# A fused attention and silu feed-forward kernel: block sums and the splits of v in another order, two silus in one, fourth sums queued behind the next first

## The chip, the cores and the metric

The kernel runs on one core of a Trainium2 chip. The metric is device time in microseconds for one execution; a kernel's time is the median over its runs.

## The reference, cut to what matters

```python
def _attn_ref(q, k, v, tau):                    # q, k, v: (2, 6016, 256) f32
    qn = q / (norm(q, axis=1) + 1e-6); kn = k / (norm(k, axis=1) + 1e-6)
    a = softmax(kn.transpose(0, 2, 1) @ qn / tau)       # (2, 256, 256): over channels
    return v @ a
def _moe_ref(x, w_in, w_out):                   # (12032, 256) @ (256, 2048) @ (2048, 256)
    h = x @ w_in
    return (h * (1 / (1 + exp(-h)))) @ w_out
```

The output is `_moe_ref(attention(q, k, v), w_in, w_out)`, a 12032 x 256 array.

## The kernel before

The attention matrix is only 256 x 256 for each of the two batches, so the kernel folds it into `w_in` (`mix`, line 433) and never forms the attention's output: tokens of v go straight into the first matmul. What is left is two matrix products with a silu between them. Both are done in a Strassen-like scheme of seven products for a 2 x 2 block product, and every f32 factor is split into a high and a low f16 half, so that one product is three matmuls (high x low, low x high, high x high).

Tokens are worked on in twelve "pairs" of up to 1024 columns (`pairs`, line 477; six for a batch, the last of a batch 896). Pairs 0 and 5 go through `emit_pair_group` (line 648), the other ten through `emit_unit` (line 706). A pair has eight units (`u` 0 to 7; the first four make the output of one half of the columns, `t` = 0, the last four the other). A unit has four slots, each ended by a `yield`:

- slot 0: products into the PSUM banks y, x and z; copies of y (`c5`) and x (`c1`) by ScalarE; `tail(0)`; the first subtraction, `top[:, 0]` = c1 - z.
- slot 1: products added to y and x; the copy `c2` of x; silu of `top[:, 0]`; `tail(1)`; the second subtraction, `top[:, 1]` = c2 - y.
- slot 2: a product (S3, T3) added to x; the third subtraction, `low[:, 1]` = x - c5; silu of `top[:, 1]`; `tail(2)`.
- slot 3: a product (A22, T4) added to x; `tail(3)`; silu of `low[:, 1]`; the last silu, from x; `high` (line 735) makes the high f16 half of the two top blocks. Then `out_of_unit` (line 795) registers what remains for later slots.

Bank x is used by four products of a unit in turn, and each one but the first needs what the one before it left to have been read.

`later(slot, ...)` (line 786) puts closures into a table by tick, a tick being one slot, and `tail` (line 780) runs those of the present tick in the order in which they were registered. For unit u these are, in the slots of unit u + 1: slot 0 `rest_top` (the low half of the top blocks, line 739, the "upper rest"), `first_sum` and `high_low`; slot 1 `rest_low` and `third_sum` (t3 = b12 + b22); slot 2 `other_sums` (t2 = t3 + b11, t4 = t2 + b21). When a half of the columns ends (u = 3 or 7) four `take`s follow in ticks 4 to 7 (ScalarE reads a finished output bank), `join` in tick 7 and two `leave`s in ticks 10 and 11 (VectorE, then a DMA on SP).

The first sum t1 = b11 + b12 and the fourth sum t4 are made by DMA: a plain DMA of the first block and an accumulating DMA of the second one, both on the POOL queue, where the second waits for the first to land (lines 910 and 911; 922 and 923). At the end of a half t4 is made by VectorE instead, and at the very end t1 too.

The output matmuls of a unit stand in the list `ready`, in passes of four matmuls with cost 4: seven in `now`, then those in `then`, which need the sums t2, t3, t1, and the fourth sum t4 of the unit before (`behind_one`). After each slot's products the main loop (line 1266) takes passes for a cost of 8, 12, 16 and 8 in slots 0 to 3. TensorE works them off in that order.

In the ten pairs the order on TensorE, VectorE and ScalarE is that of the program (`tc.manual_schedule`, line 1217); pairs 0 and 5 are ordered by the scheduler. POOL and SP each have a queue of their own.

In the background `scale_v` (line 490) prepares the next pair's v: the maximum of its absolute values by four reductions (line 518, `amax_of`), a scale (`pow2_scale`, one small matmul), sums and differences of v's blocks in f32, and the splits (`put`, line 523, by lines 163 and 165: ScalarE makes the high half, VectorE in the same step the low one). Each `yield` is a step; lines 1275 to 1278 take one in slots 0, 2 and 3 of units 1 to 7. In pairs 1 to 3 `square_sums` (line 246) runs one square of k or q in slot 1 (line 1282). In pair 0 the weights are decoded (`decode`, line 188) with a scratch tile from the room of six g buffers that the unit's blocks use too.

## Time and profile before

| | us |
|---|---|
| median of 3 runs | 1072.84 |
| lowest and highest run | 1068.92, 1073.32 |
| the profiled execution, its own time | 1070.59 |
| its span, first to last instruction | 1068.8 |
| TensorE busy in the span | 1017.0 |
| VectorE busy in the span | 826.9 |
| ScalarE busy in the span | 811.4 |

All rows below are of the profiled execution. Times are microseconds from the start of the span. PE is TensorE, DVE VectorE, ACT ScalarE, POOL GpSimd, SP SyncE; L719 is line 719 of the kernel. Names like `x<-m,wall` are tiles: what is written, and what it is made of. "Idle before" is the time for which an engine stood still ahead of an instruction, and behind the arrow stands what ended it. Ends of matmuls are modelled.

### The profile page before, as it was taken

To read this page: it belongs to the slowest core of one execution; us is meant where nothing else is said; L and a number is where in the kernel's file an instruction comes from. 1 tells how busy PE (TensorE), PEld (TensorE's weight loads), DVE (VectorE), ACT (ScalarE), POOL (GpSimd) and SP (SyncE) were. 2 spreads that over 40 slices of the span, in tenths; PEclk is the share of its full clock that TensorE was granted. 3 is DMA by queue.
4 is the path that set the end of the run, shared out by engine and by line. 5 is a ranking of instruction groups with operands and counts; after the bars stand their busy time and mean duration, and the time that the engine had idled before them with its cause. 6 is when DMAs were issued, how large, how long until landed. Compare 5 with 4: busy or idle time off the path is not lost.

```text
span 1068.8 us, 20527 instructions
## 1 busy us (share of the span) xinstructions
PE 1017.0 (95%) x8222; PEld 839.8 (79%) x8222; DVE 826.9 (77%) x1358; ACT 811.4 (76%) x1241; POOL 210.5 (20%) x301
## 2 busy tenths in 40 slices
PE   9999999998999999999999999999999999999986
PEld 8876545887888888887655787888888888888985
DVE  6998486777878778878778878878878878877764
ACT  6688596887887788778778677777777777777763
POOL 1011000222222222222000122222222222222331
PEclk9999999999999999999999999999999999999998
DMA  9995010647647556435200346435435445445443
GB/s 369 396 399 174 1 40 4 189 117 230 157 121 234 141 130 177 119 80 159 50 1 5 120 95 163 101 99 158 119 88 151 119 99 142 116 96 125 110 110 82
DMA packets 62897, 143.81 MB, mean 135 GB/s; under 512 B 6930, under 2 KB 19314, under 8 KB 62802
## 3 DMA queue, kind: packets, MB, share of 16 engines
q0 software_dynamic: 32048, 73.02, 29.3%
q1 hardware_dynamic: 30466, 68.95, 18.1%
q8 instruction: 64, 1.05, 0.4%
q10 hardware_dynamic: 288, 0.52, 0.1%
q14 instruction: 31, 0.25, 0.1%
HBM read 57.67 MB, written 12.32 MB: 65 GB/s over the span
## 4 chain that ended last, share of the span: by engine, by line
PE 50%; DVE 16%; ACT 14%; issue 10%; DMA 7%; POOL 2%; POOLq 0%; DVEq 0%; ACTq 0%
PE o L830 18%; PE x L719 10%; PE o L627 5%; PE sc L300 5%; PE y L719 4%; DVE hl L739 4%; ACT hl L736 4%; DVE g L726 4%; DMA sums<-t 3%; DMA sums<-hl 3%; ACT g L729 3%; ACT m L163 2%; PE x L658 2%; PE z L719 2%; DVE t L904 2%
## 5 line engine op out<-in xcount | busy, mean ns | idle before, releaser
L719 PEld LDWEIGHTS <-wall 128*128 128x128 f16 x3360 | 327.5, 98 | 67.6 <-issue 32.4
L719 PE MATMUL x<-m,wall 128*128 128x256 f16 (+1 forms) x1920 | 259.1, 271 | 22.0 <-DVE g L726 13.9
L739 DVE SCALAR_TENSOR_TENSOR hl<-g,sg,hl 128x1024 f16<-128x1024 f32 (+1 forms) x160 | 202.7, 1267 | 67.1 <-ACT hl L736 66.2
L830 PE MATMUL o<-hl,wo 128*128 128x256 f16 (+1 forms) x1920 | 248.5, 273 | 0.8 <-DVE hl L739 0.8
L830 PEld LDWEIGHTS <-wo 128*128 128x128 f16 x2240 | 220.0, 98 | 25.9 <-issue 1.1
L729 ACT ACTIVATE g<-g,alpha 128x512 f32<-128x512 f32 (+1 forms) x240 | 170.1, 716 | 86.0 <-DVE g L726 85.7
L736 ACT ACTIVATE hl<-g,sg 128x1024 f16<-128x1024 f32 (+1 forms) x160 | 181.6, 1136 | 0.0
L719 PE MATMUL y<-m,wall 128*128 128x256 f16 (+1 forms) x960 | 129.6, 271 | 0.1
L911 POOL DMA_DIRECT2D sums<-hl x79 | 67.9, 859 | 248.8 <-DMA sums<-hl 191.9
L910 POOL DMA_DIRECT2D sums<-hl x79 | 55.0, 697 | 264.1 <-DVE hl L739 99.4
L923 POOL DMA_DIRECT2D sums<-hl x60 | 53.8, 896 | 198.2 <-ACT hl L736 30.2
L756 ACT COPY c<-x 128x512 f32<-128x512 f32 (+1 forms) x80 | 46.3, 579 | 54.8 <-PE x L719 53.9
L627 PE MATMUL o<-hl,wo 128*128 128x512 f16 (+1 forms) x384 | 87.2, 366 | 0.0
L830 PEld LDWEIGHTS <-ws_hi 128*128 128x128 f16 x640 | 62.7, 98 | 26.7 <-issue 19.9
L164 DVE SCALAR_TENSOR_TENSOR m<-v_t,sv,m 128x512 f16<-128x512 f32 (+2 forms) x46 | 34.9, 761 | 56.5 <-ACT m L163 56.3
L729 ACT ACTIVATE g<-x,alpha 128x512 f32<-128x512 f32 (+1 forms) x80 | 54.3, 679 | 30.3 <-PE x L719 28.7
L830 PE MATMUL o<-t,ws_lo 128*128 128x256 f16 (+1 forms) x320 | 76.7, 271 | 0.0
L830 PE MATMUL o<-t,ws_hi 128*128 128x256 f16 (+1 forms) x320 | 76.7, 271 | 0.0
L300 PE MATMUL sc<-kq_t 128*128 128x256 f32 x320 | 73.1, 380 | 0.2 <-DMA kq_t<-in_kq 0.2
L726 DVE TENSOR_TENSOR g<-x,c 128x512 f32<-128x512 f32 (+1 forms) x80 | 54.4, 680 | 21.9 <-PE x L719 21.9
L627 PEld LDWEIGHTS <-wo 128*128 128x128 f16 x384 | 37.6, 98 | 39.0 <-issue 0.8
L300 PEld LDWEIGHTS sc<-kq_t 128*128 128x128 f32 x320 | 60.2, 190 | 10.2 <-DMA kq_t<-in_kq 0.8
(188 smaller groups left out, 1627.8 us busy)
## 6 DMA issues: line engine op xcount, KB each, us to landing
sums<-hl POOLq DMA_DIRECT2D x212, 256.0 KB, 3.3
kq_t<-in_kq SPq DMA_DIRECT2D x39, 512.0 KB, 8.0
sums<-t POOLq DMA_DIRECT2D x54, 256.0 KB, 3.4
v_t<-in_vT SPq DMA_DIRECT2D x10, 1024.0 KB, 5.4
outT<-sb SPq DMA_DIRECT2D x40, 256.0 KB, 2.9
turned<-in_qT SPq DMA_DIRECT2D x10, 512.0 KB, 4.5
turned<-in_kT SPq DMA_DIRECT2D x10, 512.0 KB, 6.2
raw<-in_w_in SPq DMA_DIRECT2D x5, 512.0 KB, 10.3
```

What stands on the lines that cost most here:

```text
L300: nc.tensor.matmul(sc[:, cb, :], t[:, i, 0, cb * P : (cb + 1) * P], t[:, i, 1, :], start=(j + i == 0 and cb == 0), stop=(j + i == J - 1), ...
L627: nc.tensor.matmul(o[:, :h], a[:, f, ee], hl[:, m, :h], start=(c == 1 and i == 0), stop=(c == NF and i == 2),)
L719: nc.tensor.matmul(bank[:, k * wide : (k + 1) * wide], mixed[b, i][:, v, a - 1], m[:, c, x, at : at + wide], start=(first and j + k == 0), ...
L726: nc.vector.tensor_tensor(out=g, in0=a[:, :h], in1=c[:, :h], op=ALU.subtract)
L729: nc.scalar.activation(out=g, in_=src, func=AF.Silu, scale=alpha)
L736: nc.scalar.activation(out=hl[:, :, 0], in_=g, func=AF.Copy, scale=sg)
L739: nc.vector.scalar_tensor_tensor(out=hl[:, :, 1], in0=g, scalar=sg, in1=hl[:, :, 0], op0=ALU.mult, op1=ALU.subtract,)
L756: nc.scalar.copy(c2[:, :h], x[:, :h])
L830: nc.tensor.matmul(o[:, side * wide : (side + 1) * wide], a, x, start=(first and j == 0), stop=(last and j == len(these) - 1), skip_group_ ...
L910: nc.gpsimd.dma_start(w1, blocks[0])
L911: nc.gpsimd.dma_start(w1, blocks[1], accum_op=ALU.add)
L923: nc.gpsimd.dma_start(t4, b21, accum_op=ALU.add)
```

## The change

- In a unit, silu of both top blocks is one instruction over 2 x 512 elements, in slot 2 behind `tail(2)`; silu of `low[:, 1]` follows it there, out of slot 3.
- `third_sum` is gone; t3 is made in `other_sums`, in slot 2, so that both later subtractions of a unit stand ahead of the block sums on VectorE.
- `later` has an order within a tick: passes of the running unit come first, takes behind them, `join` and `leave` last. `leave` moves from ticks 10 and 11 to 7 and 8.
- The DMAs of a unit's fourth sum are kept in `fourths` and issued in the next unit's `first_sum`: first half of t1, first half of t4, second half of t1, second half of t4. The pass that reads the earlier fourth stands ahead of the pass that reads t1. In the second half of the last pair unit 6 too makes t4 on VectorE.
- `scale_v` for pairs from 2 on takes two maxima over 1024 elements instead of four over 512, and in each step VectorE makes the low half of what ScalarE split one step earlier, together with the next sum or difference. It has 15 steps, which run in units 2, 3, 4, 6 and 7: in slots 1 to 3 in pairs 1 to 3, in slots 0 to 2 from pair 4 on. The squares of pairs 1 to 3 move to slot 0.
- `decode` takes its scratch tile from the four `sb` buffers, not from the g room.

```diff
@@ decode
-        t = room("g")[:, : k * n].bitcast(U32).rearrange("p (k n) -> p k n", k=k)
+        t = hp.tile([P, k, n], U32, tag="sb", name="t", bufs=4)
@@ scale_v
-            amax = yield from amax_of([v[kc][l] for kc in range(KC) for l in range(2)], "av")
+            amax = yield from amax_of([t[:, kc, :w] for kc in range(KC)], "av")
...
+        def high(o, src):
+            nc.scalar.activation(out=m[:, 0, o, :h], in_=src, func=AF.Copy, scale=s)
+        def low(o, src):
+            nc.vector.scalar_tensor_tensor(
+                out=m[:, 1, o, :h], in0=src, scalar=s, in1=m[:, 0, o, :h], op0=ALU.mult,
+                op1=ALU.subtract,
+            )
+        def sub(o, a, b):
+            nc.vector.tensor_tensor(out=o, in0=a, in1=b, op=ALU.subtract)
+        if p > 1:
+            high(B11, v[0][0])
+            sub(t3, v[0][1], v[1][1])
+            yield
+            low(B11, v[0][0])
+            high(B21, v[1][0])
+            yield
+            low(B21, v[1][0])
+            high(B22, v[1][1])
+            yield
+            low(B22, v[1][1])
+            sub(v[0][1], v[0][0], v[0][1])
+            yield
+            high(T1, v[0][1])
+            nc.vector.tensor_tensor(out=t2, in0=v[1][1], in1=v[0][1], op=ALU.add)
+            yield
+            low(T1, v[0][1])
+            high(T3, t3)
+            yield
+            low(T3, t3)
+            sub(t4, t2, v[1][0])
+            high(T2, t2)
+            yield
+            low(T2, t2)
+            high(T4, t4)
+            yield
+            low(T4, t4)
...
@@ emit_unit
         nc.scalar.copy(c2[:, :h], x[:, :h])
-        silu(top[:, 0], top[:, 0])
         tail(1)
         minus(top[:, 1], c2, y)
         yield
         product(x, S3, T3)
         minus(low[:, 1], x, c51[:, 0])
-        silu(top[:, 1], top[:, 1])
         tail(2)
+        silu(top, top)
+        silu(low[:, 1], low[:, 1])
         yield
         product(x, A22, T4)
         tail(3)
-        silu(low[:, 1], low[:, 1])
         silu(x[:, :h], low[:, 0])
@@ tail, later
-        for run in tails.pop(ticks[0], ()):
+        for _, run in sorted(tails.pop(ticks[0], ()), key=lambda x: x[0]):
             run()
...
-    def later(slot, *those):
-        tails.setdefault(ticks[0] + slot, []).extend(those)
+    def later(slot, *those, order=0):
+        tails.setdefault(ticks[0] + slot, []).extend((order, run) for run in those)
...
+    fourths = []
@@ out_of_unit
-        last = end and t and p == len(pairs) - 1
+        over = t and p == len(pairs) - 1
+        last = end and over
+        own = end or (over and q == 2)
...
             add("b", 0, cross(-3, 1, t3), end),
+            *behind_one,
             add("b", 1, cross(-1, 1, t1), end),
-            *behind_one,
         ]
         behind_one[:] = []
-        if end:
+        if own:
             then.append(fourth)
...
             nc.gpsimd.dma_start(w1, blocks[0])
+            for o, x, y in fourths:
+                nc.gpsimd.dma_start(o, x)
             nc.gpsimd.dma_start(w1, blocks[1], accum_op=ALU.add)
-
-        def third_sum():
-            plus(t3, b12, b22)
+            for o, x, y in fourths:
+                nc.gpsimd.dma_start(o, y, accum_op=ALU.add)
+            fourths[:] = []
 
         def other_sums():
             ready.extend(now)
+            plus(t3, b12, b22)
             plus(t2, t3, b11)
-            if end:
+            if own:
                 plus(t4, t2, b21)
             else:
-                nc.gpsimd.dma_start(t4, t2)
-                nc.gpsimd.dma_start(t4, b21, accum_op=ALU.add)
+                fourths.append((t4, t2, b21))
             ready.extend(then)
 
-        later(1, rest_low, third_sum)
+        later(1, rest_low)
         later(2, other_sums)
         if end:
             for k, name in enumerate("cabd"):
-                later(4 + k, lambda name=name: take(name))
-            later(7, join)
-            later(10, lambda: leave(0))
-            later(11, lambda: leave(1))
+                later(4 + k, lambda name=name: take(name), order=1)
+            later(7, join, lambda: leave(0), order=2)
+            later(8, lambda: leave(1), order=2)
@@ the main loop
-                if i >= 1 and vgen is not None and (
-                    p == 0 or slot in ((0, 2, 3) if p in paired else (0, 2) if not last else (0, 2, 3) if i > 4 else (2, 3))
+                if p in paired:
+                    if i in (2, 3, 4, 6, 7) and slot in ((1, 2, 3) if p < 4 else (0, 1, 2)):
+                        vgen = background(vgen)
+                elif i >= 1 and vgen is not None and (
+                    p == 0 or slot in ((0, 2) if not last else (0, 2, 3) if i > 4 else (2, 3))
                 ):
                     vgen = background(vgen, 2 if p == 0 else 1)
...
-                if p in (1, 2, 3) and sqgen is not None and slot == 1:
+                if p in (1, 2, 3) and sqgen is not None and slot == 0:
```

## Rows read from the trace of the kernel before

**Rows 1.** Page, part 1: busy us, share of the span, instructions of each engine.

```profile
PE 1017.0 (95%) x8222; PEld 839.8 (79%) x8222; DVE 826.9 (77%) x1358; ACT 811.4 (76%) x1241; POOL 210.5 (20%) x301
```

**Rows 2.** Waits, whole span: us in total, times, longest us.

```profile
POOL sums L911 <- DMA sums<-hl: 191.9, 60, 6.6
...
DVE m L164 <- ACT m L163: 66.8, 44, 3.0
...
PE o L830 <- DMA sums<-hl: 17.3, 12, 4.5
...
PE x L719 <- DVE g L726: 13.9, 27, 1.5
...
PE x L719 <- ACT g L729: 6.2, 9, 0.8
```

**Rows 3.** Timeline, TensorE, first groups of two units in a row: start, us, what.

```profile
666.04 0.82 PE L719 MATMUL y<-m,wall 128*128 128x256 f16 x6
...
675.43 0.82 PE L719 MATMUL y<-m,wall 128*128 128x256 f16 x6
```

**Rows 4.** Timeline, units 5 and 6 of pair 6; idle before in brackets.

```profile
645.34 1.80 DVE L889 TENSOR_TENSOR sb<-sb 128x256 f32<-128x256 f32 x4
...
646.45 0.81 PE L719 MATMUL x<-m,wall 128*128 128x256 f16 x6 [0.76 <-ACT g L729]
...
648.08 0.75 DVE L164 SCALAR_TENSOR_TENSOR m<-v_t,sv,m 128x512 f16<-128x512 f32 x1 [0.94 <-ACT m L163]
...
648.75 1.28 DVE L739 SCALAR_TENSOR_TENSOR hl<-g,sg,hl 128x1024 f16<-128x1024 f32 x1
...
649.94 0.68 DVE L726 TENSOR_TENSOR g<-c,z 128x512 f32<-128x512 f32 x1
...
652.46 0.69 DVE L904 TENSOR_TENSOR t<-hl 128x1024 f16<-128x1024 f16 x1
653.06 0.68 DVE L726 TENSOR_TENSOR g<-c,y 128x512 f32<-128x512 f32 x1
...
653.66 0.68 DVE L726 TENSOR_TENSOR g<-x,c 128x512 f32<-128x512 f32 x1
...
654.40 0.82 PE L719 MATMUL x<-m,wall 128*128 128x256 f16 x6 [0.56 <-DVE g L726]
```

**Rows 5.** First sum's DMAs by line: issue ns min/median/max; last, line 911's landings.

```profile
L910 POOL DMA_DIRECT2D sums<-hl x79: 554/614/1051, 191.2 to 1045.6; - x79
...
L911 POOL DMA_DIRECT2D sums<-hl x79: 853/856/893, 196.8 to 1051.4; - x79
...
DMA to landing us min/median/max: 3.2/3.3/7.9
```

**Rows 6.** The end: timeline; last, windows view (granted clock third from the end).

```profile
1041.77 1.15 DVE L739 SCALAR_TENSOR_TENSOR hl<-g,sg,hl 128x896 f16<-128x896 f32 x1 [1.48 <-ACT hl L736]
...
1045.56 1.04 POOL L910 DMA_DIRECT2D sums<-hl  x1
...
1054.74 0.35 PE L830 MATMUL o<-sums,ws_lo 128*128 128x224 f16 x1 [4.45 <-DMA sums<-hl]
...
1061.02 0.26 PE L830 MATMUL o<-t,ws_lo 128*128 128x224 f16 x1
...
1054.70:1068.80 14.10, 8.35 (x56) 7.02 (x55) 3.26 (x7) 2.54 (x4) 1.21 (x1) 0.74 0.23 55
```

**Rows 7.** Groups by line: shapes, count, busy us and mean ns, idle before.

```profile
L736 ACT ACTIVATE hl<-g,sg 128x1024 f16<-128x1024 f32 (+1 forms) x160 | 181.6, 1136 | 0.0
L729 ACT ACTIVATE g<-g,alpha 128x512 f32<-128x512 f32 (+1 forms) x240 | 170.1, 716 | 86.0 <-DVE g L726 85.7
...
L147 DVE TENSOR_REDUCE av<-v_t 128x1 f32<-128x512 f32 (+1 forms) x40 | 26.4, 664 | 0.0
```

**Rows 8.** Timeline of pair 0: a cast on ScalarE, and the product behind its queue.

```profile
78.93 0.78 ACT L202 CAST g<-wall 128x512 f16<-128x512 bf16 x1 [2.12 <-POOL g L198]
...
86.37 0.81 PE L658 MATMUL x<-m,wall 128*128 128x512 f16 x3 [2.29 <-ACT c L664]
```

More of the change, by code (lines that the diff above doesn't have):

```diff
@@ L530, in scale_v @@
         t2, t3, t4 = (x[:, i, :h] for i in range(3))
-        if p != 1:
+        def high(o, src):
[34 more added lines that the diff above has]
+            low(T4, t4)
+        if p == 0:
             put(B11, v[0][0])
             yield
-        nc.vector.tensor_tensor(out=t3, in0=v[0][1], in1=v[1][1], op=ALU.subtract)
-        yield
-        nc.vector.tensor_tensor(out=v[0][1], in0=v[0][0], in1=v[0][1], op=ALU.subtract)
-        yield
+        if p < 2:
+            sub(t3, v[0][1], v[1][1])
+            yield
+            sub(v[0][1], v[0][0], v[0][1])
+            yield
         if p == 1:
@@ L551, in scale_v @@
             yield
-        else:
+        elif p == 0:
             put(B21, v[1][0])
@@ L562, in scale_v @@
             yield
-            if p:
-                put(T3, t3)
-                yield
-                put(T2, t2)
-                yield
-                put(T4, t4)
-                yield
         while "in" not in weights:
```

## The prediction

> **What bounds the kernel now.** I read the page's busy table first: TensorE is busy for 95% of the span [rows 1], so the change can only pay where TensorE stands still. All such gaps together are what it can win, and the view of waits lists them by cause [rows 2]. Two kinds matter. TensorE waits for block sums that the POOL queue makes by DMA: 17.3 us in 12 waits. And its next product into bank x waits until VectorE or ScalarE has read the bank: 13.9 us in 27 waits and 6.2 us in 9. The same view shows what stands behind them: the POOL queue waits 191.9 us for its own first half-sums to land before it may add the second half, and VectorE waits 66.8 us at the splits of v for the high half that ScalarE makes in the same step.
>
> Then I read the timeline. A quiet unit starts 9.39 us after the one before it [rows 3]: its 42 product and 44 output matmuls are bound by TensorE, 0.109 us each. Busy units are longer, and one of them shows why [rows 4]. In unit 6 of pair 6 VectorE runs the join of the finished outputs, waits 0.94 us for a high half, and is from then on back to back: rest, subtraction, another step of v, rest, block sum, subtraction, subtraction. The last one releases bank x, and TensorE has waited 0.56 us for it. A six-matmul group lasts 0.82 us by the model, while the next one may start 6 x 0.109 = 0.655 us after it, so each wait also costs about 0.16 us of drained pipe.
>
> **The change, part by part.** Times are starts: an instruction of VectorE lets the next begin after 1.20 us (rest), 0.60 (subtraction, block sum, step of v), 0.67 (low half), 1.73 (join) [rows 4]. All terms are taken off the profiled execution, 1070.59 us (span 1068.8); that is 0.2% under the median of the runs, 1072.84.
>
> *Fourth sums behind the next first; own fourth in the last pair.* Before, each unit sends four DMAs on the POOL queue in two dependent pairs, and each second one waits for its first to land, 191.9 / 60 = 3.2 us each [rows 2]; second halves land in 3.3 us typically and 7.9 at most [rows 5]. With issue times of 0.6 to 0.9 us [rows 5] and some 2.6 us of wait behind them that is 2 x (0.7 + 2.6 + 0.86) = 8.3 us of queue at best in a unit of 9.39, and one slow landing makes it late for several units. After, the two firsts go out together and share one wait: about 0.7 + 0.86 + 2.5 + 2 x 0.86 = 5.8 us. All DMAs stay; the fourth's pair only starts half a unit later, and it is wanted half a unit after the first sum's issue plus one unit. From the end of a unit's upper rest (about 2.4 us into the next unit, by the order of work) to the output pass that reads the fourth sum (one unit of 9.39, 38 matmuls or 4.15, and one pass or 0.44 into it) there are 11.6 us, for 0.86 us of issue and two landings: two landings of up to 5.35 us fit. So the 12 waits go: 17.3 + 12 x 0.16 = 19.2 us. The last of them stands at the end [rows 6]: 4.45 us, after which the matmuls start 0.17 us apart instead of 0.095 (0.109 x 224 / 256 columns), with a granted clock of 0.74 in the last stretch. The 36 matmuls from 1054.74 to 1061.02 took 6.28 us where 36 x 0.095 = 3.4 is normal: another 2.8 us that a shorter wait gives back. What is late next: the fourth sum of unit 5, whose second DMA would go out 0.9 us behind the first sum's. The first DMA goes out when the upper rest ends, at 1042.9 instead of 1045.56, the fourth's 1.04 behind it, and two landings of 3.8 us (an estimate: somewhat over the median, since two share the engines) end at 1051.6. TensorE runs dry at 1050.3: 1.3 us stay. For slow landings in pairs 1 to 4, where other loads run, I leave 1.5 us. Gain 19.2 + 2.8 - 1.3 - 1.5 = **19.2 us**; bounds 0 (see the rivals) and 22.
>
> Second halves land here in 3.2 to 7.9 us [rows 5]. The Trainium skill (DMA: Bandwidth & Descriptors, Anatomy of one DMA) puts a DMA issued by POOL at about 2.0 us and the bytes over 436 GB/s, so 2.6 us for 256 KB, an estimate; and no second half is that fast. By that figure the 1.3 us at the end would go as well and the sum come to 1035; the sum goes by the rows.
>
> *Block sums behind both subtractions; v's halves a step apart; passes first.* In [rows 4] the block sum (0.60 us) stood ahead of both subtractions, and the wait was 0.56 us: moved behind them, that wait goes. The low half of v no longer follows its high half in the same step, so 0.94 us in front of the upper rest goes too. The steps are now 15, in slots 0 to 2 of units 2, 3, 4, 6 and 7. What is late next is found by adding up VectorE for the new order. TensorE wants the third subtraction 72 matmuls into a unit, at +7.86. In unit 6: the take of the last output ends at about +8.6 of unit 5 (ScalarE's order in slots 2 and 3), join and first leave run to +1.55 of unit 6; rest 2.75, second leave 3.35, subtraction 3.95, low half and subtraction of v 5.22, rest 6.42, subtraction 7.02, addition of v 7.62, third subtraction done 8.30. 0.5 us too late. In unit 2 the same start meets two maxima over 1024 elements. That operation is not in the trace; 512 take 664 ns [rows 7], so one is between 0.66 and 1.33 us; since elements weigh more than the start of an instruction (two silus of 716 ns against 1136 for 1024) I take 1.10 from start to start: 3.95, 5.05, 6.25, 6.85, 7.95, done 8.63. 0.83 us too late. Units 3, 4 and 7 come out between 6.9 and 7.3: no wait. So a steady pair keeps 1.3 us where it now has four waits, in units 5 to 7 (two stand in [rows 4]), at the mean of 20.1 / 36 = 0.56 us each [rows 2] and 0.16 of drained pipe: 2.9 us. Bank x waits hold 20.1 + 36 x 0.16 = 25.9 us in all; the five pairs 6 to 10 have 5 x 2.9 = 14 of them and keep 6.5. The other 12 are in pairs 1 to 4 and where an empty output queue starts (pairs 1 and 6). There the square moves to slot 0 and meets the take of an output on ScalarE: c2 then ends 0.4 us after TensorE wants it in unit 5. The softmax of the second attention fills pair 4. I let half of the 12 stay. Gain 25.9 - 6.5 - 6 = **13.4 us**; bounds 0 (all waits return elsewhere) and 22.
>
> *Two silus in one.* Two of 716 ns become one of 1024 elements, so between 716 and 1432 ns; nearest is the high half over 1024, 1136 ns [rows 7], which I take. ScalarE saves 0.3 us a unit, but it is not the bound. The merged one starts when the second subtraction is done, near +5.7, ends +6.8, the lower one +7.7, and the last silu needs the product that ends at +8.7: hidden by 1 us. Cost and gain nothing; if the second subtraction comes 1 us late, the last silu and so bank x of the next unit follow it.
>
> *Output order in the queue.* Putting the earlier fourth ahead of the first sum's pass gives that sum 0.44 us more; counted above. Takes, joins and leaves stand behind the passes of their slot, and leaves three ticks earlier: on SP's queue only the next v load follows, and no engine waits for an output that has left. Nothing, hidden by 1 us of slack in slot 3; the VectorE time of join and leave is in the sums above.
>
> *Own decode room.* At 86.37 TensorE waits 2.29 us for a copy on ScalarE, which had lost 2.12 us at 78.93 to a memset that waits for a g buffer [rows 8], and is busy from there on. With a room of its own the memset is early. VectorE is nearly full there too, so between 0 and 2.45; I take **2.0 us**, since the two numbers are so near.
>
> Sum: 19.2 + 13.4 + 2.0 = 34.6; 1070.6 - 34.6 = **1036 us**.
>
> **Rivals.** *VectorE becomes the bound (chance 0.17).* The steps of v are packed into 5 of 8 units. For it: unit 6 adds up to 9.0 of 9.39 us of VectorE; any further delay goes straight to TensorE. Against: it has no waits on ScalarE in that order. Then the bank x waits stay as they are: 1036 + 13.4 + 2 = about 1051.
>
> *The POOL queue was not late because of its own waits (0.10).* If landings are slowed by other traffic, the sums are as late as now. For: the 7.9 us landing. Against: the longest of the 12 waits, 4.45 us, is at the end, where nothing is loaded any more [rows 6]. Then 1070.6 - 13.4 - 2 = 1055.
>
> *Slower: two pairs in flight land too late (0.04).* Place: every unit, the pass of the fourth sum, which stands in front of all others in the in-order TensorE. It decides when the mean landing passes 5.35 us, the slack above. With 6 us it is 2 x 0.65 = 1.3 us a unit, some 60 units: 1036 + 78 = 1114. For: 7.9 us was seen. Against: the median is 3.3. 79 issues on line 911 took 853 to 893 ns beside a VectorE at work [rows 5], so nothing held them up. The Trainium skill (SBUF — State Buffer, SBUF: two separate sides) names a way to such a delay, a VectorE operation in a fast two-port mode that keeps GpSimd from writing descriptors; by that rule the moved DMAs could be late, and these rows do not bear it out, so it has no chance beyond the 0.04.
>
> *It does not do what it says (0.02):* TensorE's gaps are where they are for other reasons; within 0.5%.
>
> **How the numbers follow.** Forecast 0.67, the others as given. The forecast's own range runs from 1024 (VectorE waits down to 3 us, the full 2.45) to 1046. The whole range, 1024 to 1052, takes in the VectorE rival and leaves out the two DMA ones and the tails. About 0.5%, 5 us, is what a measurement of this kernel can tell from no change: faster 0.92 (forecast, VectorE and late POOL rivals, 0.94, less 0.02 for cases where both of these meet), same 0.03, slower 0.05.
>
> **What would show it.** Right: no waits of the output passes on block sums before the end, and under 2 us there, a clock near 1 in the last 14 us; one wait of line 911's place in the POOL queue per unit, shared with the fourth; steady pairs 1.5 us shorter, with their remaining waits in units 2 and 6; no VectorE wait at the low halves of v. Wrong: waits of the output passes for the fourth sum in every unit, or bank x waits of 20 us and more as now.

## The result, and the profile after

The changed kernel takes 1062.51 us (median of 9 runs, 1056.94 to 1067.44) against 1071.73 us of the kernel before beside it: a ratio of 0.9914, interval 0.9887 to 0.9941. It is faster, by about a quarter of what was forecast, and lies outside the range given. The profiled execution took 1060.87 us (span 1059.1) against 1070.59 (1068.8). Line numbers below are those of the changed kernel: the products are L753 (before L719), the output passes L866 (L830), the rest L773 (L739), the subtractions L760 (L726), the first sum's DMAs L946 and L949 (L910, L911), the fourth's L948 and L951 (L922, L923).

The page, part 1, of the kernel after, beside [rows 1]:

```profile
PE 1015.2 (96%) x8222; PEld 841.5 (79%) x8222; DVE 831.7 (79%) x1339; ACT 800.8 (76%) x1161; POOL 207.7 (20%) x299
```

TensorE stands still for 1059.1 - 1015.2 = 43.9 us, where before it was 1068.8 - 1017.0 = 51.8. So 7.9 of the 9.7 us came out of gaps. The view of waits says which (beside [rows 2]; us in total, times, longest us):

```profile
POOL sums L949 <- DMA sums<-hl: 206.6, 57, 8.9
...
POOL sums L951 <- DMA sums<-t: 48.4, 13, 8.9
...
PE o L866 <- DMA sums<-hl: 22.9, 10, 4.4
...
PE x L753 <- ACT c L790: 3.5, 6, 1.6
...
PE x L753 <- DVE g L760: 2.6, 6, 0.8
...
PE x L753 <- ACT g L763: 2.0, 1, 2.0
```

In the kernel before, one more line of that view belongs to bank x, its waits for a copy by ScalarE:

```profile
PE x L719 <- ACT c L756: 1.3, 2, 0.7
```

The two halves of the change went opposite ways. With the waits for a copy counted on both sides, the waits for bank x fell from 20.1 + 1.3 = 21.4 us in 38 to 2.6 + 3.5 + 2.0 = 8.1 us in 13, as forecast. The waits for block sums, which should have gone, grew from 17.3 to 22.9 us; and the POOL queue waits for its own landings as much as before, 206.6 us for 191.9.

The timeline of unit 6 of a steady pair (it starts at 799.21) shows the half that worked, beside [rows 4]: the join, the third subtraction and the product that needs it.

```profile
798.06 1.86 DVE L925 TENSOR_TENSOR sb<-sb 128x256 f32<-128x256 f32 x4
...
806.50 0.68 DVE L760 TENSOR_TENSOR g<-x,c 128x512 f32<-128x512 f32 x1
...
807.23 0.81 PE L753 MATMUL x<-m,wall 128*128 128x256 f16 x6
```

VectorE runs from the join to the third subtraction without a bracket, so without a wait, and no block sum stands between, and TensorE's product into bank x carries no bracket: its unit takes 9.55 us (the next starts at 808.75), where a quiet one has 9.39.

The timeline of units 6 and 7 of pair 7 and unit 0 of pair 8 (they start at 721.28, 730.83 and 740.22) shows the half that did not:

```profile
724.35 0.69 POOL L946 DMA_DIRECT2D sums<-hl  x1
728.68 0.84 POOL L949 DMA_DIRECT2D sums<-hl  x1 [3.64 <-DMA sums<-hl]
731.15 0.57 POOL L948 DMA_DIRECT2D sums<-t  x1 [1.62 <-DVE t L940]
...
734.79 0.69 DVE L542 TENSOR_TENSOR x<-x,v_t 128x512 f32<-128x512 f32 x1
...
735.55 0.38 SPq L485 DMA_DIRECT2D v_t<-in_vT  x1
735.88 0.84 POOL L951 DMA_DIRECT2D sums<-hl  x1 [4.17 <-ACT c L790]
736.62 0.67 POOL L946 DMA_DIRECT2D sums<-hl  x1
743.98 0.84 POOL L949 DMA_DIRECT2D sums<-hl  x1 [6.69 <-DMA sums<-hl]
...
747.30 0.27 PE L866 MATMUL o<-sums,ws_lo 128*128 128x256 f16 x1 [1.89 <-DMA sums<-hl]
```

The order is 946, 949, 948, 951: both DMAs of the first sum, then both of the fourth. That is the old order. The two firsts do not go out together, and a unit can still have two waits for a landing (3.64 and 4.17 us here; the second is listed under a copy on ScalarE, but 951 begins 0.5 us after the landing of 948 at 735.36). And something new stands in it: v's next load goes out at 735.55, right after the last instruction that reads the old v (L542, in unit 7). The 946 behind it takes 7.1 us to land (743.69), so 949 is late, and TensorE waits 1.89 us.

### The profile page after: what moved, and what is told of

It is laid out like the page before. It is cut to its first block, busy times and chain, and to the rows that moved or that the text cites. A ratio compares the mean times of both kernels' runs of the same rounds, so it can differ in the third digit from the quotient of the medians.

```text
span 1059.1 us, 20486 instructions
## 1 busy us (share of the span) xinstructions
PE 1015.2 (96%) x8222; PEld 841.5 (79%) x8222; DVE 831.7 (79%) x1339; ACT 800.8 (76%) x1161; POOL 207.7 (20%) x299
## 5 line engine op out<-in xcount | busy, mean ns | idle before, releaser
L753 PEld LDWEIGHTS <-wall 128*128 128x128 f16 x3360 | 328.4, 98 | 49.4 <-issue 12.9
L753 PE MATMUL x<-m,wall 128*128 128x256 f16 (+1 forms) x1920 | 260.7, 272 | 8.4 <-ACT c L790 3.5
L773 DVE SCALAR_TENSOR_TENSOR hl<-g,sg,hl 128x1024 f16<-128x1024 f32 (+1 forms) x160 | 203.0, 1269 | 76.1 <-ACT hl L770 74.8
L866 PE MATMUL o<-hl,wo 128*128 128x256 f16 (+1 forms) x1920 | 248.7, 273 | 0.5 <-DVE hl L773 0.5
L866 PEld LDWEIGHTS <-wo 128*128 128x128 f16 x2240 | 220.3, 99 | 27.9 <-issue 2.9
L763 ACT ACTIVATE g<-g,alpha 128x1024 f32<-128x1024 f32 (+3 forms) x160 | 146.0, 927 | 88.7 <-DVE g L760 86.5
L753 PE MATMUL y<-m,wall 128*128 128x256 f16 (+1 forms) x960 | 129.8, 271 | 0.1
L949 POOL DMA_DIRECT2D sums<-hl x79 | 67.2, 851 | 278.7 <-DMA sums<-hl 206.6
L946 POOL DMA_DIRECT2D sums<-hl x79 | 57.9, 733 | 227.7 <-DMA outT<-sb 103.8
L951 POOL DMA_DIRECT2D sums<-hl x59 | 51.8, 878 | 184.9 <-DMA sums<-t 48.4
L760 DVE TENSOR_TENSOR g<-x,c 128x512 f32<-128x512 f32 (+1 forms) x80 | 54.5, 681 | 42.6 <-PE x L753 42.5
L866 PEld LDWEIGHTS <-ws_hi 128*128 128x128 f16 x640 | 62.9, 98 | 29.8 <-issue 23.0
L866 PE MATMUL o<-t,ws_lo 128*128 128x256 f16 (+1 forms) x320 | 76.7, 271 | 0.0
L866 PE MATMUL o<-t,ws_hi 128*128 128x256 f16 (+1 forms) x320 | 76.7, 271 | 0.0
L760 DVE TENSOR_TENSOR g<-c,y 128x512 f32<-128x512 f32 (+1 forms) x80 | 54.3, 679 | 28.3 <-ACT c L790 27.8
## 6 DMA issues: line engine op xcount, KB each, us to landing
raw<-in_w_in SPq DMA_DIRECT2D x5, 512.0 KB, 10.5
```

Of the source, the lines that this page charges most:

```text
L753: nc.tensor.matmul(bank[:, k * wide : (k + 1) * wide], mixed[b, i][:, v, a - 1], m[:, c, x, at : at + wide], start=(first and j + k == 0), ...
L760: nc.vector.tensor_tensor(out=g, in0=a[:, :h], in1=c[:, :h], op=ALU.subtract)
L763: nc.scalar.activation(out=g, in_=src, func=AF.Silu, scale=alpha)
L773: nc.vector.scalar_tensor_tensor(out=hl[:, :, 1], in0=g, scalar=sg, in1=hl[:, :, 0], op0=ALU.mult, op1=ALU.subtract,)
L866: nc.tensor.matmul(o[:, side * wide : (side + 1) * wide], a, x, start=(first and j == 0), stop=(last and j == len(these) - 1), skip_group_ ...
L946: nc.gpsimd.dma_start(w1, blocks[0])
```

## Experiments

All ratios are to the kernel before on the same chip (median 1073.21 us for the first four runs, 1072.96 for the next four, 1070.79 for the last two).

**The POOL queue in program order.** Source and queue differ because the ten pairs keep program order only on TensorE, VectorE and ScalarE; POOL is left to the scheduler. The first DMAs of POOL's queue as they are emitted:

```
changed kernel:      946 949 | 948 951 | 946 949 | 948 951 ...
with POOL in order:  946 949 | 946 948 949 951 | 946 948 949 951 ...
```

```diff
-                        mybir.EngineType.PE, mybir.EngineType.DVE, mybir.EngineType.Activation
+                        mybir.EngineType.PE, mybir.EngineType.DVE, mybir.EngineType.Activation,
+                        mybir.EngineType.Pool
```

> The changed kernel with POOL added to the engines that keep program order. Theory A (the POOL queue's order is the scheduler's, so the fourth sums never went behind the next first): the queue now runs first, fourth's first, second, fourth's second; the output passes' waits on sums fall from 22.9 us in 10 waits to under 5 us, and with the half clock behind them gone the time is 1035 to 1045 us. Theory B (landings are slow because v's load and other loads fall on them): the waits stay over 15 us and the time stays at 1057 to 1067 us.

Measured: 1043.34 us, ratio 0.9745 (0.970 to 0.979), some 19 us below the changed kernel and in the range of theory A, though the waits for sums fell to 9.6 us and not under 5. Of the spans' difference, 1059.1 - 1042.0 = 17.1 us, 13.3 are waits for sums and 3.6 TensorE's busy time (1015.2 and 1011.6 in the page). Waits:

```profile
POOL sums L949 <- DMA sums<-hl: 159.1, 72, 5.6
...
PE o L866 <- DMA sums<-hl: 9.6, 6, 3.3
...
POOL sums L951 <- DMA sums<-t: 2.2, 3, 1.2
```

Timeline of the same place, units 6 and 7 of pair 7 (unit 7 starts at 723.43):

```profile
716.96 0.57 POOL L946 DMA_DIRECT2D sums<-hl  x1 [6.11 <-PE z L753]
717.51 0.56 POOL L948 DMA_DIRECT2D sums<-t  x1
720.19 0.88 POOL L949 DMA_DIRECT2D sums<-hl  x1 [2.12 <-DMA sums<-hl]
720.97 0.99 POOL L951 DMA_DIRECT2D sums<-hl  x1
726.77 0.57 POOL L946 DMA_DIRECT2D sums<-hl  x1 [4.82 <-issue]
...
728.15 0.38 SPq L485 DMA_DIRECT2D v_t<-in_vT  x1
```

One round takes 721.96 - 716.96 = 5.0 us and the queue then rests for 4.82. Where 951 waited 48.4 us in 13 for its own first half, 2.2 in 3 are left. First halves of the first sum land after a median of 2.3 us (the changed kernel: 3.6). v's load goes out at unit 7 + 4.7 here too, but both firsts have gone by then, and no output pass waits. What is left of the waits of the output passes stands at the end (2.04 us) and from pair 2 to the start of pair 5 (7.6 us), now for the fourth sum.

**The changed kernel without the fourth-sum part:** the fourth's DMAs issued in `other_sums` and its pass placed as before, own fourth in the last unit alone.

```diff
-        own = end or (over and q == 2)
+        own = end
...
@@ other_sums
-                fourths.append((t4, t2, b21))
+                nc.gpsimd.dma_start(t4, t2)
+                nc.gpsimd.dma_start(t4, b21, accum_op=ALU.add)
```

> The changed kernel without its part on fourth sums (fourth DMAs issued in other_sums as before, pass order as before, unit 6 of the last pair by DMA again). Theory A: the POOL order is the same as in the changed kernel, so the time is 1058 to 1068 us, the same within the scatter. If that part did act: 1072 to 1085 us. Theory B says nothing on it.

Measured: 1066.12 us, ratio 0.9956 (0.9919 to 0.9992); waits for sums 26.0 us in 13. The interval overlaps that of the changed kernel. So its fourth-sum part, as it was emitted, was worth about 1066.12 - 1062.51 = 3.6 us, the own fourth of the last pair included; the scatter hardly tells that from nothing, and it is not 19.2.

**The kernel before, with the fourth-sum part alone, in program order** (the pass order and the own fourth of unit 6 in the last pair belong to it):

```diff
...
+            for o, x, y in fourths:
+                nc.gpsimd.dma_start(o, x)
             nc.gpsimd.dma_start(w1, blocks[1], accum_op=ALU.add)
+            for o, x, y in fourths:
+                nc.gpsimd.dma_start(o, y, accum_op=ALU.add)
+            fourths[:] = []
...
@@ engines={
+                        mybir.EngineType.Pool
```

> The kernel before with the part on fourth sums alone, and POOL in program order. Theory A: the waits on sums (17.3 us in 12 waits, and the half clock at the end) go, bank x waits stay at 20 us: 1049 to 1057 us. Theory B: 1068 to 1074 us.

Measured: 1082.0 us, ratio 1.0093 (1.0063 to 1.0123): slower, so theory A missed on its sign, and theory B gave 1074 us at most. The waits for sums are longer in all than in any other run, and those of the ten pairs stand at the fourth sum, most of them in unit 7:

```profile
PE o L833 <- DMA sums<-hl: 28.1, 13, 5.8
```

Timeline, units 6 and 7 of pair 7 (739.36 and 750.41); here 913, 915, 916, 918 are the round of four DMAs:

```profile
745.17 0.57 POOL L913 DMA_DIRECT2D sums<-hl  x1 [7.64 <-DVE g L726]
745.72 0.56 POOL L915 DMA_DIRECT2D sums<-t  x1
745.79 0.38 SPq L485 DMA_DIRECT2D v_t<-in_vT  x1
...
752.88 0.86 POOL L918 DMA_DIRECT2D sums<-hl  x1 [4.06 <-DMA sums<-t]
...
757.22 0.60 PE L833 MATMUL o<-sums,wo 128*128 128x256 f16 x4 [2.06 <-DMA sums<-hl]
```

In unit 6 the upper rest is late (the join and the wait for a high half stand before it, [rows 4]), so the round begins 5.8 us into the unit and not 3.1. With v's steps as before, v's load goes out right then. The fourth's first half lands after 6.87 us, its second half goes out 2.5 us into unit 7 and lands at 757.18; TensorE wanted it at 755.16.

**In order, with the decode in the g room again**, the one line of `decode` in the diff turned back.

> As the first of these runs, but decode takes its scratch from the g room again. If the own room is worth what was forecast, 2 us slower than that run; since the wait of 2 us near 86 us is still there in the changed kernel, I expect it within 1 us of that run, the wait at 86 us between 1.9 and 2.4 us in both.

Measured: 1045.67 us, ratio 0.9749 (0.9712 to 0.9785), against 0.9745 with a room of its own. The medians differ by 2.3 us, the ratios by 0.0004, or 0.4 us, and the runs of either kernel scatter by 5 us and more: in time the room is worth nothing that can be told. The wait near 86 us is 2.2 us here and 1.96 with the room.

**In order, with the loads of the squares on ScalarE's queue**, so that they are not held behind v's load on SP and sent in a bunch:

```diff
-            nc.sync.dma_start(t[:, : w - u], (qT, kT)[i][cb * P : (cb + 1) * P, u:w])
+            nc.scalar.dma_start(t[:, : w - u], (qT, kT)[i][cb * P : (cb + 1) * P, u:w])
```

> As the run with POOL in program order (1043.3 us), but the loads for the squares go out from ScalarE's queue, not behind v's load on SP's. Theory C: what is left of waits on sums in pairs 2 and 3 (7.2 us in 4 waits, and a half clock after the longest) comes from three 512 KB loads that SP's queue holds behind v's load and then sends at once: these waits fall under 3 us and the time is 1037 to 1041 us. Theory D (v's load alone, or traffic in general): no change, 1041 to 1046 us.

Measured: 1041.86 us, ratio 0.9718 (0.9695 to 0.9742); waits for sums 9.2 us in 6, where 9.6 were. The bunch is not what makes them; whether the 1.5 us are a gain is open.

**In order, without the squares of the second batch:** no loads of q and k and no squares in pairs 1 to 3, the sums set to 1. The kernel leaves that work out.

```diff
-            nc.sync.dma_start(t[:, : w - u], (qT, kT)[i][cb * P : (cb + 1) * P, u:w])
...
-            nc.scalar.activation(
-                out=sq[:, : t.shape[1]], in_=t, func=AF.Square, accum_out=sum_
-            )
+        nc.vector.memset(m, 1.0)
+        for _ in range(25):
             yield
```

> As the run with POOL in program order, but without the squares of the second batch and their 24 loads (the norms are constants: this part of the computation is left out). Theory C and theory D in its form of traffic in general: no waits on sums in pairs 1 to 3, 1033 to 1038 us. If v's load alone slows the landings: waits of 2 us and more stay in pairs 2 and 3, 1039 to 1044 us.

Measured: 1033.94 us, ratio 0.9644 (0.9622 to 0.9666). The time is in the range of "traffic in general", but waits for sums stay, in 6 places again, and shorter:

```profile
PE o L852 <- DMA sums<-hl: 6.9, 6, 1.8
```

The longest stands in unit 0 of pair 2, 1.84 us, where no load but v's is on its way; the next, 1.75, in unit 0 of pair 3. In the first of these the second half of the fourth went out 0.56 us ahead of v's load and landed after 9.45 us. So v's load alone can cost 1.8 us. In pairs 6 to 10, where v's steps run a slot earlier, it costs 0.6 us at most: this made the place of v's load a suspect by itself (the last two runs). Of the 1042.0 - 1031.5 = 10.5 us of span that went with the squares and their loads, the waits for sums are only 9.6 - 6.9 = 2.7; 5.0 are TensorE's busy time (1011.6 and 1006.6) and 2.2 the waits for c2 (3.5 and 1.3). The run takes ScalarE's work away together with the loads, so it does not tell the two apart.

**As the ScalarE-queue version, with the last sums on VectorE:** in the last pair units 5 and 6 make t4 and unit 6 also t1 on VectorE.

```diff
-        own = end or (over and q == 2)
+        own = end or (over and q >= 1)
-            if last:
+            if over and q >= 2:
                 plus(t1, b11, b12)
```

> As the run with the squares' loads on ScalarE's queue, and in the last pair VectorE also makes the fourth sums of units 5 and 6 and the first sum of unit 6. The wait of 2.0 us at the end is for the fourth sum of unit 5: it goes, and with it the half clock that follows it in the last 5 us: 3 to 4 us faster than that run. If VectorE's extra 1.8 us in units 6 and 7 hold up bank x instead, no gain.

Measured: 1040.37 us, ratio 0.9702 (0.9684 to 0.972); waits for sums 8.3 us in 8. The wait at the end went from 2.28 to 1.01 us and is now one for the rest (L773). The gain over its base, 1.5 us, is less than was expected and within the scatter. The edit acts in the last pair alone, yet the wait in unit 0 of pair 2 is 1.10 us, where its base had 2.72, and unit 7 of pair 1 has one of 1.56, where the base had none: single waits of the earlier pairs differ by 1.6 us from one profile to another. In pair 2, unit 7 (322.41), the load of v meets the second halves at 7.4 us, and the longest wait follows in unit 0 of pair 3:

```profile
329.77 0.38 SPq L485 DMA_DIRECT2D v_t<-in_vT  x1
...
330.49 1.14 POOL L951 DMA_DIRECT2D sums<-hl  x1
...
339.56 1.01 PE L866 MATMUL o<-sums,wo 128*128 128x256 f16 x4 [3.01 <-DMA sums<-hl]
```

**In order, with v's splits and their places as before:**

```diff
-                if p in paired:
-                    if i in (2, 3, 4, 6, 7) and slot in ((1, 2, 3) if p < 4 else (0, 1, 2)):
-                        vgen = background(vgen)
-                elif i >= 1 and vgen is not None and (
+                if i >= 1 and vgen is not None and (
```

(with the splits, maxima and squares that belong to it, as in the diff of the change, turned back)

> As the run with POOL in program order, but with v's splits and their places in the units as before. Theory E: the kernel before with the fourth part alone was slower (1082 us) since in unit 6 the first sum's DMA waits for an upper rest that stands behind the join and a split's wait on ScalarE, while v's load falls on its landing; then the sums' waits in unit 7 are back, 4 to 6 us in pairs 1 to 3: 1055 to 1075 us. If instead the joins and leaves ahead of the passes did it, which this run has moved, there are no such waits: 1043 to 1050 us.

Measured: 1079.54 us, ratio 1.0054 (1.0027 to 1.0082), above the 1055 to 1075 of theory E, whose waits are back. Waits:

```profile
PE o L832 <- DMA sums<-hl: 27.0, 11, 4.9
```

and timeline, units 6 and 7 of pair 7 (unit 7 starts at 748.65):

```profile
743.53 0.57 POOL L912 DMA_DIRECT2D sums<-hl  x1 [7.27 <-DVE sb L895]
...
744.75 0.38 SPq L485 DMA_DIRECT2D v_t<-in_vT  x1
...
755.24 0.60 PE L832 MATMUL o<-sums,wo 128*128 128x256 f16 x4 [1.65 <-DMA sums<-hl]
```

The same picture as in the kernel before with the fourth-sum part: a late round in unit 6, v's load on top of it, a wait in unit 7. The new queue order pays only together with v's new steps, which bring the round of unit 6 forward (from + 5.6 to + 3.1) and push v's load back behind both firsts (from unit 6 + 6.8 to unit 7 + 4.7).

**As the version with the last sums on VectorE, with v's steps in slots 0 to 2 in all pairs:**

```diff
-                    if i in (2, 3, 4, 6, 7) and slot in ((1, 2, 3) if p < 4 else (0, 1, 2)):
+                    if i in (2, 3, 4, 6, 7) and slot in (0, 1, 2):
```

> The version with the last sums on VectorE, with v's steps in slots 0 to 2 in all pairs (in pairs 1 to 3 they were in slots 1 to 3); the squares stay in slot 0. Place theory: the waits in unit 0 of pairs 2 and 3 (3 us and more there, 1.8 without the squares) come from v's load going out at unit 7 + 7.3, on top of the two second halves, where in pairs 6 to 10 it goes out at + 4.7 and nothing waits. By it the load moves to about + 4.7 in pairs 1 to 3 and the waits for block sums fall from 8.3 to 3 to 4.5 us; the time comes to 1034 to 1038, unless the square and a step of v in the same slot make ScalarE late, which then shows as waits for c2 growing from 2.8 us to 5 and more (time as before, 1040). Rival (the load costs its wait wherever it stands in pairs 1 to 3, because the other loads of these pairs are what counts): waits for block sums stay at 7 to 9 us, 1039 to 1042.

Measured: 1033.3 us, ratio 0.9643 (0.9618 to 0.9667): the best of all versions that do the whole work. Waits:

```profile
PE o L866 <- DMA sums<-hl: 1.9, 3, 1.0
```

Timeline, the same place as in the version before (unit 7 of pair 2 starts at 321.13, and no wait for a sum follows):

```profile
325.85 0.38 SPq L485 DMA_DIRECT2D v_t<-in_vT  x1
...
329.65 1.11 POOL L951 DMA_DIRECT2D sums<-hl  x1
```

v's load goes out 4.7 us into the unit. The second half of the fourth now takes 5.3 us and not 9.0, and the wait of 3.01 us in unit 0 of pair 3 is gone. In unit 0 of pair 2 the second half takes 6.8 us and not 9.0, but the wait there stays, 1.02 us for 1.10, since TensorE gets there sooner. Over the span the waits for sums fall from 8.3 to 1.9 us, and the waits for c2 do not grow (2.8 to 2.2). The rival's ranges are missed, in waits and in time, and the place theory's (3 to 4.5 us and 1034 to 1038) are bettered by a little. Of the 6.4 us of waits, though, 1.56 and 1.29 stood in unit 7 of pair 1 (ahead of v's load) and in unit 3 of pair 3, where v's load is not seen to be the cause. That its place makes the wait is shown for pair 3; that it makes all of the 7 us is not, since all of v's steps moved with it.

**The same, with the squares of pairs 1 to 3 in slot 3:**

```diff
-                if p in (1, 2, 3) and sqgen is not None and slot == 0:
+                if p in (1, 2, 3) and sqgen is not None and slot == 3:
```

> As the one before, with the squares of pairs 1 to 3 in slot 3, so that no square meets a step of v on ScalarE. Place theory: waits for block sums 3 to 4.5 us as there; waits for c2 no more than the 2.8 us of the base; 1032 to 1037. Against: a square in slot 3 (716 ns and more on ScalarE) stands in front of the last silu and of the high half, so bank x (waits on the silu of line 763, 2.0 us now) and the rest come later in 25 units; at 0.3 us each that would be 7 us and 1043 to 1046. Rival (other loads count, not v's place): 1039 to 1042 with waits for block sums of 7 to 9 us.

Measured: 1041.9 us, ratio 0.9727 (0.9702 to 0.9751). It is slower than with the squares in slot 0, but not in the way given, and in the rival's range of time: the wait for the silu stays at 2.0 us, while sums take 6.3 us in 7 and one copy of y in pair 4 holds TensorE for 3.3. ScalarE's timeline there:

```profile
417.08 0.95 ACT L265 ACTIVATE sq<-turned 128x896 f32<-128x896 f32 x1 [2.42 <-DMA turned<-in_kT]
...
418.03 0.57 ACT L780 COPY c<-y 128x512 f32<-128x512 f32 x1
```

A square whose load has not landed holds up the copy that the next unit's bank y needs. The sums come later too, and v's load has moved again. At the start of unit 7 of pair 1 (244.27) the square stands ahead of the copies on ScalarE, the first subtraction waits 0.60 us for one of them, and v's last reader comes after it:

```profile
249.69 0.38 SPq L485 DMA_DIRECT2D v_t<-in_vT  x1
...
261.20 0.60 PE L866 MATMUL o<-sums,wo 128*128 128x256 f16 x4 [1.39 <-DMA sums<-hl]
```

The load goes out at + 5.4 there and at + 5.5 in pair 2, where it was + 4.7; the second half of the fourth takes 9.2 us again in pair 1, and the waits in unit 0 of pairs 2 and 3 are 1.39 and 1.81 us. In unit 0 of pair 3 the three runs go with the load's place: 3.01 us at + 7.4, 1.81 at + 5.5, none at + 4.7. In unit 0 of pair 2 they do not: 1.10, 1.39 and 1.02. So this run fits the place theory in one of the two places and does not decide between it and the rival.

## Why the prediction was wrong

**The bound.** TensorE's gaps were the right place to look, and every microsecond above was won or lost in them, in the drained pipe behind them or in TensorE's clock.

**Fourth sums: the step that failed** is "After, the two firsts go out together and share one wait". It was read off the source. The queue of POOL is not emitted in the order of the source, and the fact was in the prediction's own material: the kernel names the engines that keep program order, and POOL is not among them. So in the changed kernel the first sum's second half waits 206.6 us in 57 for its first and the fourth's 48.4 in 13, and the output passes wait 22.9 us, where the sum left 1.3 + 1.5 = 2.8. The mechanism was there to be had: with POOL in order the round takes 5.0 us (5.8 forecast) and the second wait is gone. Its size, though, was too large for the change as written. From the kernel before to the in-order one the waits for sums fall by 17.3 - 9.6 = 7.7 us, and 6 waits fewer at 0.16 us of drained pipe make 1.0 more. TensorE's busy time falls by 1017.0 - 1011.6 = 5.4 us, but drained pipe is in it, (6 + 25) x 0.16 = 5.0 us with the waits for bank x below, so the clock gives back 0.4 us and not 2.8: the end runs faster (the windows below), while the granted clock is 0.50 from 339.72 to 346.55, in and behind the wait of 3.33 us. That is 7.7 + 1.0 + 0.4 = 9.1 of the 19.2 us. The 1.3 us left for the end were 2.04, and the 1.5 us left for slow landings in pairs 1 to 4 were 7.6. With v's steps a slot earlier in pairs 1 to 3, and so its load, and with the last sums on VectorE, 1.9 us of such waits are left in all, and the kernel takes 1033.3 us, where 1036 was forecast for the change.

**What the prediction did not cost** is where v's load goes. It said that only the next v load follows the leaves on SP's queue, and took that as harmless. Moving the last reader of v from unit 6 to unit 7 moved the load too, and in the old queue order it falls on the next unit's first sum (the timeline after, 735.55 to 747.30). In the profiles the waits for sums grew by 5.6 us. Those in a unit 0, which now follow v's load closely, grew from 2.4 us (1.72 and 0.70) to 11.5 (3.35, 1.92, 4.38 and 1.89); all others fell from 14.9 to 11.4. The clock went with them: in and behind each of the three longest (3.35, 4.38 and 4.38 us) there is a stretch at a granted clock of 0.50, the lower of its two levels (1.2 GHz), where the kernel before has one at the wait at its end alone (1053.76 to 1060.59). The longest is in pair 3, windows view:

```profile
345.89:356.13 10.24, 5.86 (x29) 4.19 (x28) 2.67 (x4) 0.72 (x1) 3.05 (x5) 0.50 0.59 162
```

TensorE's busy time fell by 1.8 us only, where 27 waits fewer at 0.16 take off 4.3, so the clock took some 2.5 us, an estimate from these rows. One of the two longest waits, 4.38 us at the end, is the one of [rows 6] once more (4.45), and so is the low clock there. Windows view of the last 15 us after, and of the same stretch in the in-order kernel (granted clock third from the end):

```profile
1044.10:1059.10 15.00, 6.45 (x52) 5.67 (x51) 4.57 (x10) 2.43 (x4) 0.00 (x0) 0.78 0.20 48
```

```profile
1027.00:1042.00 15.00, 6.67 (x68) 6.25 (x66) 7.35 (x12) 4.18 (x6) 0.00 (x0) 0.92 0.21 47
```

**Bank x: right, and undersized.** Forecast 13.4 us; the rows give 21.4 - 8.1 = 13.3 and 25 waits less at 0.16, so 17.3. VectorE's 66.8 us at the splits of v are gone from the view of waits. How much of the gain they brought is not shown: with v's splits and steps as before (the eighth run) the waits for bank x are 7.2 us in 13 too, so the new order of block sums, passes and silus is enough for it there, though the output passes of that slower kernel wait 6.5 us in 10 for a rest, where the changed kernel has 0.5 in 2. The third subtraction of unit 6 starts 7.29 us into the unit and ends at + 7.97 (forecast 8.30). Unit 2 was right as to its place and too dear by 0.45 us; timeline of pair 9, unit 2 (836.92):

```profile
840.54 1.21 DVE L147 TENSOR_REDUCE av<-v_t 128x1 f32<-128x1024 f32 x1
841.67 1.27 DVE L773 SCALAR_TENSOR_TENSOR hl<-g,sg,hl 128x1024 f16<-128x1024 f32 x1
...
845.32 0.82 PE L753 MATMUL x<-m,wall 128*128 128x256 f16 x6 [0.38 <-DVE g L760]
```

The unseen maximum over 1024 elements lets the next instruction begin after 1.13 us; 1.10 was taken. Pair 9 takes 75.9 us (818.14 to 894.01), where it took 78.4: 2.5 us shorter, not 1.5.

**Two silus in one: nothing, but for one place.** It takes 1149 ns (1136 forecast) and is covered. The one wait for it, 2.0 us, is in the softmax of pair 4: a function table is loaded before the exponentials (at 470.69) and again before the silu, 1.28 us each, and the silu that reads bank x stands behind them, the merged one and a split of v (L533, at 476.06). The longest wait of this kind was 0.8 us before. The merging alone does not make it: with the silus merged and v's steps as before (the eighth run) this wait is 0.74 us. Timeline of ScalarE, after:

```profile
473.10 1.28 ACT L763 ACT_TABLE_LOAD   x1
...
476.62 0.67 ACT L763 ACTIVATE g<-x,alpha 128x512 f32<-128x512 f32 x1
```

**The own decode room: 0.3 and not 2.0 us.** TensorE still waits 1.97 us at 86.42 for the copy on ScalarE, where it waited 2.29. A cast still waits for a memset, 1.25 us at 78.82, where one had lost 2.12, and ScalarE is busy for 6.37 of the 6.40 us from 80.0 to 86.4: the memset was one of several things in its way, and its own work is the bound.

**The rivals.** That the POOL queue was not late because of its own waits (1055) came nearest in time and is not the reason: with the waits shared, 19 us went. What it says of other traffic is borne out in part by what is left (the runs without the squares and with v's steps earlier). "Two pairs in flight land too late" does happen, in the kernels whose round of unit 6 meets v's load, with first halves of the fourth that take 6.87 us (pair 7 of the third run) against the 5.35 at which it was to decide; those kernels are 6 to 10 us slower than the one before, not 43, since from pair 6 on it happens once in a pair. VectorE did not become the bound: TensorE's waits for its subtractions fell from 13.9 to 2.6 us. The chance of faster was right in its sign, for the part of it that rested on bank x.

**Open:** how much of what is left between the in-order kernel and the best version is the place of v's load, how much the other loads and how much ScalarE's work on the squares; and whether one more buffer for v (`load_v` has three), with its load sent far earlier, would take the last 1.9 us. No run shows either.

## What to carry to other kernels

An order written in the source is an order on a queue only if that queue keeps it: before costing a move on a DMA queue, look which engines the schedule holds to program order, and in the profile at the sequence of that queue's rows. And when the last reader of a buffer moves, ask which load waits for it, and on whose landings that load will then fall. Two parts may also need each other: here the new queue order without v's new steps was slower than the kernel before, twice.

## What was not expected of the hardware

**Landings.** A 256 KB DMA from the POOL queue, SBUF to SBUF, landed after 2.3 us (plain, the median of line 946 in order) or 3.4 (accumulating, line 949 there). With a 1 MB load of v beside it, an accumulating one took 4.69 us in one place (329.00 in the run with v's steps in slots 0 to 2) and 9.45 in another (249.61 in the run without the squares), and 10.2 where 512 KB loads for the squares ran too (330.68 in the run with POOL in order). The Trainium skill (DMA: Bandwidth & Descriptors, Anatomy of one DMA) gives about 2.0 us and the bytes over 436 GB/s, by which 256 KB take an estimated 2.6 us. The median of the plain DMA is 0.3 us under that and the accumulating one 0.8 over it; with a load beside it the measurement decides.

**The clock.** Two kernels wait equally long for the same product in pair 0, 1.97 us in the changed kernel and 1.96 with POOL in order. Windows view of the 3.6 us behind it, in this order (granted clock third from the end):

```profile
86.40:90.00 3.60, 3.58 (x9) 2.51 (x9) 3.60 (x9) 3.60 (x6) 0.52 (x1) 0.53 0.97 381
```

```profile
86.40:90.00 3.60, 3.26 (x15) 2.26 (x15) 3.60 (x9) 3.60 (x7) 0.52 (x1) 1.00 0.96 373
```

The granted clock is 0.53 in the first, near the lower of its two levels, 1.2 GHz, and 1.00, the higher one, 2.4 GHz, in the second. In both TensorE was busy without a gap from 80.00 to 84.45, ahead of the wait, at a granted clock of 1.00; and behind the wait of 2.29 us of the kernel before [rows 8] the clock stayed at 1.00 as well (86.37 to 90.00). No row looked at tells them apart, so a wait of 2 us may or may not cost some 3.6 x 0.47 = 1.7 us more, an estimate, which may be part of the scatter of these kernels.
